# Attention, SwiGLU and four experts on one core: weight scaling, state decay, loads, first-stage order and last sums rearranged

## The chip, the cores and the metric

The kernel runs on one core of one Trainium2 chip. A core has five engines that work side by side, each through its own instructions in their order: PE (TensorE, matmuls, with its weight loads shown as PEld), DVE (VectorE), ACT (ScalarE), POOL (GpSimd) and SP (SyncE, which issues DMAs here). They wait for each other by semaphores. Data lies in DRAM, in on-chip SBUF (128 partitions) and in the eight banks of PSUM that PE adds into. The metric is the time of one execution on the device in microseconds (us), median of the runs.

## The reference

Three parts follow one another on 2 batches of 768 tokens with 384 channels (8 heads of 48), in float32:

```python
for t in range(S):                                   # attention with a decaying state
    state = alpha[:, :, t, :, None] * state + np.einsum('bhd,bhe->bhde', k[:, :, t], v[:, :, t])
    y[:, :, t] = np.einsum('bhd,bhde->bhe', q[:, :, t], state)

rms = np.sqrt(np.mean(x * x, axis=-1, keepdims=True) + 1e-06)
xn = x / rms * rms_g                                 # norm with a gain per channel
g = xn @ w_gate                                      # 384 x 1536
silu = g * (1.0 / (1.0 + np.exp(-g)))
x2 = silu * (xn @ w_val) @ w_out                     # 1536 x 384

p = domain_probs / (domain_probs.sum(-1, keepdims=True) + 1e-09)
for e in range(E):                                   # four experts, all of them used
    h = np.maximum(x2 @ w1[e], 0.0)                  # 384 x 1024
    out += p[:, e:e + 1] * (h @ w2[e])               # 1024 x 384
```

## The kernel before

**Products.** A float32 product is made of three matmuls in PE's faster format (`mm3`, L918 to L920): every operand is split into a high part (a rounded copy) and a low part (what is left), and low x high, high x high, high x low are added in one PSUM bank. So each weight and each intermediate needs a high copy (`whi`, `hh`, `x1h`, on ACT) and a subtraction (`wlo`, `hl`, `x1l`, on DVE).

**Attention.** Time is cut into six chunks c of 128 steps, for two batches b. Of a chunk the kernel loads alpha (`af`), k and q (`kq`, two DMAs of 224 KB, L617) and v, forms decay products by scans on DVE (`a_prep`, L652, L663, scaling the key at L679), scores on PE and a mask on DVE (`a_score`, L715, L724), the output (`a_y`, L735), the state S of each batch (`a_state`: the key's transpose L767, its copy `kdT` on ACT, the products L781, the decay of S by one DVE multiply, L812, and the addition, L807), and the norm without gain (`a_rms`), which leaves `x1h` and `x1l`.

**SwiGLU.** Tokens go in three blocks of 512 (`block1`). Of each block twelve steps f follow: a gate and a val product of nine matmuls each (`up1`, banks `g`, two of them), silu and the product with val, the split into `hh` and `hl`, and an output product of nine matmuls into three banks `o` (`outs`), one step behind. Block 0 needs chunks 0 and 1; its first four f run in two halves of 256 tokens, since chunk 1 is worked on at the same time. The last `outs` of a block comes directly behind the one before it.

**Weights.** Eighteen units of 128x768 (gate, val, out in turn, units u % 3 = 0, 1, 2) hold the SwiGLU weights. Each is loaded as 64-bit words (768 KB, L479, two buffers `raw`) and turned into float32 by three DVE operations (`w_conv`: L575, L583, L591, two buffers `cv`). `hilo_first` splits it: gate and val units are scaled by the gain `gneg` of the norm in three pieces on ACT (L514) and again in three pieces in the DVE subtraction (L526); out units need one ACT copy (L511) and one subtraction (L521). For units 0 to 2 the low part is made on PE instead (L543, L551) and copied by ACT (L558).

**Experts.** For each of four experts, three blocks and eight f: an up product (`e_up`, nine matmuls, banks `g` and `ph`), relu and split (L1266 on ACT, L1271 on DVE), a down product of nine matmuls into the three banks `o` (`e_down`). After f = 7 each bank is multiplied by the token's probability (L1314) and added to `acc` (L1322), in whole rows of 512 columns for experts 0 to 2, in halves of 256 for expert 3, which then stores each half from SP (L1330).

**Order.** A list scheduler (class `Plan`) sets the order of all engines' instructions when the program is built, from costs in us, handover times and a bias for each group of operations (`BIAS`); `MARGIN` and `SLIP` say when an operation may wait for a better one. Where the plan leaves PE idle ahead of the first dense product, `idle` (L1064 to L1070) puts in matmuls on zeros, of which there are 35 in groups of 20, 5, 5 and 5. The experts are planned with other, unchanged settings.

## Time and profile before

| | us |
|---|---|
| median of three runs | 706.62 (706.56 to 707.48) |
| the profiled execution | 706.30 |
| its span (first to last instruction) | 704.6 |
| PE busy | 688.9 (98%) |
| DVE busy | 323.9 (46%) |
| ACT busy | 199.2 (28%) |
| POOL busy | 13.0 (2%) |

Busy time counts an engine's work alone; an engine that waits in its order for a semaphore is idle. A timeline row gives the start in us from the span's start, the length in us, engine, line, operation, out<-in and the number of instructions that were put together; in brackets the idle time before it and what ended it. The length of a group reaches from the first start to the last end, and one matmul's or vector operation's length overlaps the next one's start, so the pace is read from the starts.

### The profile page before, as it was taken

How to read it: one execution, taken by the hardware profiler on the slowest of the kernel's cores; microseconds unless marked ns; L12 is line 12 of the kernel's file. 1: busy time of each engine (PE TensorE's matmuls, PEld its weight loads, DVE VectorE, ACT ScalarE, POOL GpSimd, SP SyncE). 2: the span in 40 equal slices, each digit the busy share in tenths (PEclk: the TensorE clock that was granted, in tenths of full speed). 3: DMA queues.
4: the chain of work that ended last, by engine and by line, in shares of the span. 5: the costliest groups of instructions: out<-in, count | busy, mean ns of one | idle time of the engine just before them, and what ended most of it. 6: DMA issues, size and time to landing. Idle time of an engine off the chain costs nothing. (4 is left out here: it accounts for less than half of the span.)

```text
span 704.6 us, 9312 instructions
## 1 busy us (share of the span) xinstructions
PE 688.9 (98%) x3877; PEld 570.7 (81%) x3877; DVE 323.9 (46%) x555; ACT 199.2 (28%) x407; POOL 13.0 (2%) x26
## 2 busy tenths in 40 slices
PE   8989999999999999999999999999999999999995
PEld 6889888778888888878888888888888888878784
DVE  7899999984223543431224413143313132231413
ACT  3754545443122443421113311113111111111110
POOL 1010000000000000000000000000000000000000
PEclk9999999999999999999999999999999999999999
DMA  9933554160000222320001210001000000000001
GB/s 260 268 130 116 172 183 151 61 214 1 1 1 2 91 93 87 124 100 1 16 0 60 93 57 16 0 16 45 16 1 15 1 15 1 16 22 23 30 16 47
DMA packets 21135, 45.16 MB, mean 64 GB/s; under 512 B 2160, under 2 KB 12192, under 8 KB 21088
## 3 DMA queue, kind: packets, MB, share of 16 engines
q1 hardware_dynamic: 20800, 44.49, 19.8%
q8 instruction: 31, 0.51, 0.3%
q14 instruction: 16, 0.13, 0.1%
q10 hardware_dynamic: 288, 0.03, 0.0%
HBM read 41.34 MB, written 3.17 MB: 63 GB/s over the span
## 5 line engine op out<-in xcount | busy, mean ns | idle before, releaser
L918 PE MATMUL o<-hl,whi 128*128 128x512 f32 (+1 forms) x408 | 158.0, 387 | 3.2 <-DVE acc L1322 1.6
L920 PE MATMUL o<-hh,wlo 128*128 128x512 f32 (+1 forms) x408 | 156.3, 383 | 0.0
L919 PE MATMUL o<-hh,whi 128*128 128x512 f32 (+1 forms) x408 | 156.2, 383 | 0.0
L918 PE MATMUL g<-x1l,whi 128*128 128x512 f32 (+1 forms) x384 | 146.5, 381 | 0.0
L920 PE MATMUL g<-x1h,wlo 128*128 128x512 f32 (+1 forms) x384 | 144.4, 376 | 0.0
L919 PE MATMUL g<-x1h,whi 128*128 128x512 f32 (+1 forms) x384 | 144.4, 376 | 0.0
L1271 DVE SCALAR_TENSOR_TENSOR hl<-g,hh 128x512 fp32r<-128x512 f32 x48 | 33.2, 691 | 146.0 <-ACT hh L1266 146.0
L918 PEld LDWEIGHTS o<-hl,whi 128*128 128x128 f32 x408 | 76.6, 188 | 20.7 <-PE ph L920 2.4
L920 PEld LDWEIGHTS o<-hh,wlo 128*128 128x128 f32 x408 | 76.6, 188 | 15.2
L919 PEld LDWEIGHTS o<-hh,whi 128*128 128x128 f32 x408 | 76.7, 188 | 14.4
L1271 DVE SCALAR_TENSOR_TENSOR hl<-ph,hh 128x512 fp32r<-128x512 f32 x48 | 33.1, 690 | 114.5 <-ACT hh L1266 114.4
L918 PEld LDWEIGHTS g<-x1l,whi 128*128 128x128 f32 x384 | 72.2, 188 | 14.0 <-DVE s L975 0.2
L920 PEld LDWEIGHTS g<-x1h,wlo 128*128 128x128 f32 x384 | 72.2, 188 | 13.3
L919 PEld LDWEIGHTS g<-x1h,whi 128*128 128x128 f32 x384 | 72.2, 188 | 12.7
L1266 ACT ACTIVATE hh<-g 128x512 fp32r<-128x512 f32 x48 | 28.7, 598 | 160.3 <-PE g L920 160.3
L1266 ACT ACTIVATE hh<-ph 128x512 fp32r<-128x512 f32 x48 | 28.7, 598 | 152.7 <-PE ph L920 152.7
L918 PE MATMUL ph<-x1l,whi 128*128 128x512 f32 x144 | 56.0, 389 | 0.0
L919 PE MATMUL ph<-x1h,whi 128*128 128x512 f32 x144 | 56.0, 389 | 0.0
L920 PE MATMUL ph<-x1h,wlo 128*128 128x512 f32 x144 | 56.0, 389 | 0.0
L975 DVE TENSOR_TENSOR s<-g,s 128x512 f32<-128x512 f32 (+1 forms) x40 | 25.4, 634 | 60.2 <-PE g L920 59.0
L493 DVE TENSOR_TENSOR wlo<-raw,whi 128x768 fp32r<-128x768 f32 x32 | 30.6, 956 | 20.4 <-ACT whi L488 20.1
L967 ACT ACTIVATE s<-g 128x512 f32<-128x512 f32 (+1 forms) x40 | 22.1, 552 | 53.0 <-PE g L920 52.6
(132 smaller groups left out, 606.1 us busy)
## 6 DMA issues: line engine op xcount, KB each, us to landing
raw<-in_w SPq DMA_DIRECT2D x34, 768.0 KB, 4.3
kq<-in_kq SPq DMA_DIRECT2D x20, 224.0 KB, 3.3
s<-p_dram SPq DMA_DIRECT2D x12, 256.0 KB, 3.5
out_y<-acc SPq DMA_DIRECT2D x18, 128.0 KB, 1.7
af<-in_af SPq DMA_DIRECT2D x10, 226.2 KB, 3.6
v<-in_v SPq DMA_DIRECT2D x10, 192.0 KB, 4.2
x_dram<-s SPq DMA_DIRECT2D x3, 256.0 KB, 3.3
raw<-x_dram SPq DMA_DIRECT2D x1, 768.0 KB, 4.2
```

The lines of the kernel that those rows point to most:

```text
L493: lambda: nc.vector.tensor_tensor(out=lo(), in0=src_ap(), in1=hi().bitcast(F32), op=ALU.subtract),
L918: nc.tensor.matmul(ps_ap, lhsT=lh, rhs=rl, start=first, stop=False)
L919: nc.tensor.matmul(ps_ap, lhsT=lh, rhs=rh, start=False, stop=False)
L920: nc.tensor.matmul(ps_ap, lhsT=ll, rhs=rh, start=False, stop=last)
L967: lambda: nc.scalar.activation(out=s()[:, :n], in_=pg()[:, :n], func=AF.Silu),
L975: lambda: nc.vector.tensor_mul(s()[:, :n], pv()[:, :n], s()[:, :n]), r=[pv], w=[s],
L1266: "ACT", 0.5, lambda: nc.scalar.activation(out=hh(), in_=ph(), func=AF.Relu),
L1271: lambda: nc.vector.scalar_tensor_tensor(out=hl(), in0=ph(), scalar=0.0, in1=hh().bitcast(F32), op0=ALU.max, op1=ALU.subtract,),
```

## The change

It has six parts.

1. The first plan has a bias for each step of each chunk (`00l` to `51y`: chunk, batch, and l, p, s, y, t or r for load, preparation, score, output, state and norm) and for each weight unit, other `MARGIN` and `SLIP`, other costs and start times. The order of the first stage becomes another. The fills are again 35, now in groups of 25, 5, 4 and 1, the first ahead of the first score.
2. Ten gate and val units (3, 4, 6, 7, 9, 10, 12, 13, 15, 16) are scaled in place on ACT before they are split; then one plain ACT copy makes the high part and one DVE subtraction the low part. Units 0 and 1 stay as they were, and buffers are tracked in halves.
3. The decay of the state is made by four ACT copies with a scale (112x96 each), for each of eight chunk-and-batch pairs, in place of one DVE multiply of 112x384.
4. k and q come in one DMA of 448 KB, but for chunk 0 of batch 0.
5. The first `e_up` is issued ahead of the last `outs` of block 2; from then on each down product follows its next up product, one step behind.
6. Expert 3 sums and stores in whole rows. Its last block has a sequence of its own (`e_end`): the third bank is closed after f = 4 and summed early; up products 6 and 7 follow; then f = 5 to 7 of the first two banks, with their sums and stores; then f = 5 to 7 of the third in two halves of 256 columns, in a `g` and a `ph` bank, each summed and stored, the last store from ACT's queue.

The diff, cut to its core (renamed keys, other costs and the table's entries are left out):

```diff
-BIAS = {"c00": -3016.7, "c01": -1212.5, "w0": 2486.8,
...
-MARGIN, SLIP = 0.00, 8.13
+BIAS = {'': -1198.5, '00l': -490.0, '00p': 390.6,
...
+MARGIN, SLIP = 8.75, 47.05
...
-            return 0.26 if b == "PE" else 0.2 if a == "PE" else 0.16
+            return 0.4 if b == "PE" else 0.2 if a == "PE" else 0.18
...
+    plan.FROM = {"SP": 0.7, "ACT": 3.3, "POOL": 2.4}
...
-        return plan.op("SP", max(0.6, mb / 0.36), fn, **kw)
+        return plan.op("SP", 0.25 + mb / 0.38, fn, **kw)
...
-        def his():
-            if not gains:
-                nc.scalar.activation(out=hi(), in_=t().bitcast(F32), func=AF.Copy)
-                return
+        def scaled(out):
             for k in range(KD):
                 nc.scalar.activation(
-                    out=part(hi(), k), in_=part(t().bitcast(F32), k), func=AF.Copy,
-                    scale=gneg[:, k : k + 1],
+                    out=part(out, k), in_=part(word(), k), func=AF.Copy, scale=gneg[:, k : k + 1]
                 )
-        def los():
...
-            for k in range(KD):
-                nc.vector.scalar_tensor_tensor(
-                    out=part(lo(), k), in0=part(t().bitcast(F32), k), scalar=gneg[:, k : k + 1],
-                    in1=part(hi().bitcast(F32), k), op0=ALU.mult, op1=ALU.subtract,
-                )
         if not by_pe:
-            plan.op("DVE", 1.0 if gains else 0.87, los, r=[t, hi], w=[lo])
+            if gains:
+                plan.op("ACT", 1.26, lambda: scaled(word()), r=key(t), w=key(t))
+            plan.op(
+                "ACT", 0.75, lambda: nc.scalar.activation(out=hi(), in_=word(), func=AF.Copy),
+                r=key(t), w=key(hi),
+            )
+            plan.op(
+                "DVE", 0.87,
+                lambda: nc.vector.tensor_tensor(
+                    out=lo(), in0=word(), in1=hi().bitcast(F32), op=ALU.subtract
+                ),
+                r=[*key(t), *key(hi)], w=key(lo),
+            )
+            return
...
+        if (c, b) == (0, 0):
...
+        else:
             dma(
-                0.23, lambda i=i: nc.sync.dma_start(out=t()[:HP, i], in_=kq[c, b, :, i]),
-                w=[(t, i)], chain=chain,
+                0.46, lambda: nc.sync.dma_start(out=t()[:HP], in_=kq[c, b]),
+                w=[(t, 0), (t, 1)], chain=chain,
             )
...
+        def scale():
+            for j in range(NP):
+                nc.scalar.activation(
+                    out=s()[:, j], in_=s()[:, j], func=AF.Copy,
+                    scale=p()[:, C + j * CS : C + j * CS + 1],
+                )
+
         if c:
-            plan.op(
-                "DVE", 0.47, lambda: nc.vector.tensor_mul(s(), s(), whole(2 * D)), r=[p],
-                w=[(s, 0), (s, 1)],
-            )
+            plan.op("ACT", 0.9, scale, r=[p], w=[(s, 0), (s, 1)])
...
-    def block1(steps, open_po=None):
+    def block1(steps, open_po=None, ahead=None):
...
+        if ahead:
+            ahead()
         outs(len(steps) - 1)
...
+    def e_end(e, blk):
+
+        e_up(e, blk, 5)
+        for d in range(KD):
+            e_prod(e, blk, 4, d, last=4 if d == 2 else 7)
+        e_sum(e, blk, 2)
+        e_up(e, blk, 6)
+        e_up(e, blk, 7)
+        for d, f in ((0, 5), (0, 6), (1, 5), (1, 6), (0, 7), (1, 7)):
+            e_prod(e, blk, f, d)
+            if f == 7:
+                e_sum(e, blk, d)
+                e_store(blk, d)
+        for c in halves:
+            pe[2] = h_bank()
+            for f in (5, 6, 7):
+                e_prod(e, blk, f, 2, c, first=5)
+            e_sum(e, blk, 2, c)
+            e_store(blk, 2, c, "ACT" if c.start else None)
...
+    for n in block1([(2, slice(0, 512), f) for f in range(12)], ahead=lambda: e_up(*es[0])):
...
-    for n, st in enumerate(es):
-        e_up(*st)
-        if n > 1:
-            if n == 2:
-                e_down(*es[0])
+    for n, st in enumerate(es[:-3]):
+        if n:
+            e_up(*st)
             e_down(*es[n - 1])
...
-    e_down(*es[-1])
+    e_end(E - 1, 2)
```

`e_prod` makes the three matmuls of one f and one bank, `e_sum` the multiplication and the addition of one bank, `e_store` the store.

Three places in the new order. The first is SP's queue in the first 25 us, where the first `raw` is weight unit 1 and the second unit 2, `wlo` and `whi` stand for chunk 1's alpha and v, and the later `af` and `kq` for chunk 2. Before:

```order
L479 DMA raw<-in_w 128x1536
L612 DMA wlo<-in_af 112x517
L628 DMA whi<-in_v 128x384
L612 DMA wlo<-in_af 112x517
L628 DMA whi<-in_v 128x384
L612 DMA af<-in_af 112x517 x2
L617 DMA kq<-in_kq 112x512
L479 DMA raw<-in_w 128x1536
L617 DMA x1h<-in_kq 112x512 x2
```

After:

```order
L480 DMA raw<-in_w 128x1536
L616 DMA wlo<-in_af 112x517
L639 DMA whi<-in_v 128x384
L616 DMA wlo<-in_af 112x517
L639 DMA whi<-in_v 128x384
L480 DMA raw<-in_w 128x1536
L616 DMA af<-in_af 112x517 x2
L627 DMA x1h<-in_kq 112x1024
```

Unit 2's load now stands ahead of chunk 2's loads, directly behind chunk 1's v. On DVE the three conversions of unit 0 (before L575, L583, L591) stand with one short operation between them; before, unit 1's first conversion stood ahead of the second, and a mask and two steps of the norm ahead of the third.

The second place is PE ahead of the first dense matmul (L918 before, L944 after). `g<-cv` and `g<-whi,nident` make the low part of units 0 to 2 in the g banks (`cv,ident` is unit 2), `att<-x1h` is the score of chunk 1, batch 0. Before:

```order
L543 MATMUL g<-cv,wlo 128x128 x3
L551 MATMUL g<-whi,nident 128x384
L1070 MATMUL o<-zw 128x512 x5
L715 MATMUL att<-x1h 128x128 x8
L543 MATMUL g<-cv,ident 128x128 x3
L551 MATMUL g<-whi,nident 128x384
L543 MATMUL g<-cv,ident 128x128 x3
L918 MATMUL g<-x1l,whi 128x256
```

After:

```order
L546 MATMUL g<-cv,wlo 128x128 x3
L554 MATMUL g<-whi,nident 128x384
L546 MATMUL g<-cv,ident 128x128 x3
L554 MATMUL g<-whi,nident 128x384
L546 MATMUL g<-cv,ident 128x128 x3
L728 MATMUL att<-x1h 128x128 x8
L944 MATMUL g<-x1l,whi 128x256
```

The split of unit 2 moves ahead of the score, and dense work follows the score directly.

The third place is DVE at the end of the program, from the last up products on. Before:

```order
L1271 SCALAR_TENSOR_TENSOR hl<-g,hh 128x512
L1271 SCALAR_TENSOR_TENSOR hl<-ph,hh 128x512
L1314 TENSOR_TENSOR o<-o,s 128x256
L1322 TENSOR_TENSOR acc_3728<-o,acc_3728 128x256
L1314 TENSOR_TENSOR o<-o,s 128x256 x3
L1322 TENSOR_TENSOR acc_3728<-o,acc_3728 128x256 x2
L1314 TENSOR_TENSOR o<-o,s 128x256 x2
L1322 TENSOR_TENSOR acc_3728<-o,acc_3728 128x256 x3
```

After:

```order
L1343 TENSOR_TENSOR o<-o,s 128x512
L1351 TENSOR_TENSOR acc_3726<-o,acc_3726 128x512
L1292 SCALAR_TENSOR_TENSOR hl<-g,hh 128x512
L1292 SCALAR_TENSOR_TENSOR hl<-ph,hh 128x512
L1343 TENSOR_TENSOR o<-o,s 128x512 x2
L1351 TENSOR_TENSOR acc_3726<-o,acc_3726 128x512 x2
L1343 TENSOR_TENSOR g<-g,s 128x256
L1343 TENSOR_TENSOR ph<-ph,s 128x256
L1351 TENSOR_TENSOR acc_3726<-g,acc_3726 128x256
L1351 TENSOR_TENSOR acc_3726<-ph,acc_3726 128x256
```

The third bank's first sum moves ahead of the last two `hl`, and behind them stand four whole-row and four half-row operations in place of twelve half-row ones.

## Rows read from the trace of the kernel before

**Rows 1.** Page, first part: busy us, share of the span and instructions of each engine.
```profile
PE 688.9 (98%) x3877; PEld 570.7 (81%) x3877; DVE 323.9 (46%) x555; ACT 199.2 (28%) x407; POOL 13.0 (2%) x26
```
**Rows 2.** Stretches: length, busy us of PE, PEld, DVE, ACT, POOL; last, GB/s.
```profile
0.00:31.20 31.20, 27.23 (x252) 22.66 (x252) 24.50 (x45) 16.44 (x48) 3.59 (x16) 1.00 0.92 265
31.20:130.00 98.80, 96.52 (x893) 83.54 (x893) 98.44 (x186) 49.74 (x129) 6.81 (x6) 1.00 0.45 146
```
**Rows 3.** PE's waits over the span: for whom, us in total, times, longest.
```profile
PE o L918 <- DVE acc L1322: 1.6, 2, 0.8
```
**Rows 4.** Timeline of PE around the first dense matmul.
```profile
28.41 1.16 PE L715 MATMUL att<-x1h 48*128 48x128 f32 x16 [0.73 <-DVE x1h L679]
...
31.20 0.38 PE L918 MATMUL g<-x1l,whi 128*128 128x256 f32 x1
```
**Rows 5.** Timeline of DVE, conversions of units 0 to 2 (the last row is unit 2's).
```profile
12.26 0.55 DVE L575 TENSOR_SCALAR cv<-raw 128x768 uint32<-128x768 uint32 x1
14.22 0.56 DVE L575 TENSOR_SCALAR cv<-raw 128x768 uint32<-128x768 uint32 x1 [1.40 <-DMA raw<-in_w]
...
16.95 0.95 DVE L591 SCALAR_TENSOR_TENSOR cv<-raw,cv 128x768 uint32<-128x768 uint32 x1
...
28.18 0.95 DVE L591 SCALAR_TENSOR_TENSOR cv<-raw,cv 128x768 uint32<-128x768 uint32 x1
```
**Rows 6.** Timeline of SP's queue: the load of unit 2.
```profile
18.06 1.21 SPq L479 DMA_DIRECT2D raw<-in_w  x1
```
**Rows 7.** Line 479 at 18 us, the same load: from issue to landing.
```profile
DMA to landing us min/median/max: 6.2/6.2/6.2
```
**Rows 8.** Line 628 from 8.5 to 9 us, chunk 1's second v load.
```profile
DMA to landing us min/median/max: 9.4/9.4/9.4
```
**Rows 9.** DVE's groups by shape: count, busy us, mean ns of one, idle before.
```profile
L526 DVE SCALAR_TENSOR_TENSOR wlo<-cv,gneg,whi 128x256 fp32r<-128x256 f32 x30 | 12.7, 480 | 0.0
...
L1314 DVE TENSOR_TENSOR o<-o,s 128x512 f32<-128x512 f32 x18 | 11.9, 690 | 0.0
...
L521 DVE TENSOR_TENSOR wlo<-cv,whi 128x768 fp32r<-128x768 f32 x5 | 4.8, 954 | 0.1
L812 DVE TENSOR_TENSOR S<-S,F 112x384 f32<-112x384 f32 x8 | 4.4, 552 | 0.0
```
**Rows 10.** ACT's groups by shape, columns as before.
```profile
L511 ACT ACTIVATE whi<-cv 128x768 fp32r<-128x768 f32 x6 | 5.1, 847 | 7.6 <-DVE cv L591 7.6
...
L558 ACT ACTIVATE wlo<-g 128x384 fp32r<-128x384 f32 x6 | 3.0, 499 | 0.6 <-PE g L551 0.6
...
L693 ACT ACTIVATE junk<-af 112x4 bf16<-112x4 f32 x10 | 2.1, 207 | 7.8 <-issue 6.0 <-DVE rms L849 0.8 <-ACT s L967 0.6
...
L1076 ACT ACTIVATE wlo<-ident,gneg 128x128 f32<-128x128 f32 x3 | 1.0, 385 | 0.0
```
**Rows 11.** Timeline of PE at the last output product of block 2.
```profile
300.27 0.50 PE L918 MATMUL o<-hl,whi 128*128 128x512 f32 x1 [0.41 <-DVE hl L985]
```
**Rows 12.** Timeline of PE where expert 3 goes from block 0 to 1.
```profile
632.92 0.39 PE L920 MATMUL ph<-x1h,wlo 128*128 128x512 f32 x1
634.10 0.47 PE L918 MATMUL o<-hl,whi 128*128 128x512 f32 x1 [0.79 <-DVE acc L1322]
...
635.45 0.39 PE L919 MATMUL o<-hh,whi 128*128 128x512 f32 x1
```
**Rows 13.** Timeline of PE, its last matmuls (seven in a row).
```profile
695.60 0.39 PE L920 MATMUL o<-hh,wlo 128*128 128x512 f32 x1
...
696.96 0.39 PE L920 MATMUL o<-hh,wlo 128*128 128x512 f32 x1
```
**Rows 14.** Timeline of DVE's last sums, the first and the last row.
```profile
696.02 0.43 DVE L1314 TENSOR_TENSOR o<-o,s 128x256 f32<-128x256 f32 x1 [1.40 <-PE o L920]
...
699.15 1.08 DVE L1322 TENSOR_TENSOR acc<-o,acc 128x256 f32<-128x256 f32 x3
```
**Rows 15.** Line 1330 from 700.4 us on, the last two stores.
```profile
DMA to landing us min/median/max: 1.8/2.2/2.6
```

More of the change, by code (lines that the diff above doesn't have):

```diff
@@ L158, in schedule @@
         ready = [0.0] * n
-        busy, cand, start = {}, {}, [None] * n
+        busy, cand, start = dict(self.FROM), {}, [None] * n
         for i in range(n):
@@ new lines, in hilo_first, with whole @@
+        if gains:
+            plan.op("ACT", 1.26, lambda: scaled(hi()), r=key(t), w=key(hi))
+        else:
+            plan.op(
+                "ACT", 0.75, lambda: nc.scalar.activation(out=hi(), in_=word(), func=AF.Copy),
+                r=key(t), w=key(hi),
+            )
+        for f in range(2):
+            p = gbank()
+            sl = slice(f * DM, (f + 1) * DM)
+            def whole(p=p, sl=sl):
+                for k in range(KD):
+                    c = slice(k * P, (k + 1) * P)
+                    nc.tensor.matmul(
+                        p()[:, c], lhsT=gdiag()[:, c] if gains else ident, rhs=word()[:, sl][:, c],
+                        start=k == 0, stop=False,
+                    )
+            plan.op("PE", 0.75, whole, r=[(t, f), gdiag], w=[p])
+            plan.op(
+                "PE", 0.2,
+                lambda p=p, sl=sl: nc.tensor.matmul(
+                    p()[:, :DM], lhsT=nident, rhs=hi()[:, sl], start=False, stop=True
+                ),
+                r=[(hi, f)], w=[p],
+            )
+            plan.op(
+                "ACT", 0.42,
+                lambda p=p, sl=sl: nc.scalar.activation(
+                    out=lo()[:, sl], in_=p()[:, :DM], func=AF.Copy
+                ),
+                r=[p], w=[(lo, f)],
+            )
@@ L578, in w_conv @@
             ),
-            r=[r], w=[t],
+            r=[r], w=key,
         )
@@ L586, in w_conv @@
             ),
[L587 removed]
+            r=[r], w=key,
         )
@@ L749, in go @@
                     inner(j, 1)
-            plan.op("PE", 1.73, go, r=[vt, *a, (Sp, 0), (Sp, 1), (t, 1)], w=[y])
+            plan.op(
+                "PE", 1.78, go,
+                r=[(vt, 0), *((x, n) for x in a for n in range(2)), (Sp, 0), (Sp, 1), (t, 1)], w=[y],
+            )
         else:
@@ L928, in dn_ops, with wr @@
         return tuple(t()[:, o + sl.start : o + sl.stop] for t in units[key])
-    def wr(u):
-        hi, lo = units[u]
-        return hi, lo, (lo, 0), (lo, 1)
+    def wr(u, f):
+        return [(t, f % 2) for t in units[u]]
     def u1(f, w):
@@ L957, in prod @@
             i = plan.op(
-                "PE", 9 * (n / 2400 + 0.0145), go, r=[*wr(u1(f, w)), *parts], w=[p], chain="dense"
+                "PE", 9 * (n / 2400 + 0.0145), go, r=[*wr(u1(f, w), f), *parts], w=[p], chain="dense"
             )
@@ L1288, in p_load, with parts, e_open, e_prod @@
         )
+    halves = (slice(0, 256), slice(256, 512))
+    def parts(t, cols, *key):
+        return [(t, *key, c.start) for c in halves if cols.start <= c.start < cols.stop]
+    def e_open(e, blk):
+        for d in range(KD):
+            pe[d] = obank()
+        p_load(e, blk)
+    def e_prod(e, blk, f, d, cols=slice(0, 512), first=0, last=7):
+        key = (19 + 4 * e + 2 * (f // 4), f // 2 % 2)
+        hh, hl = hq[e, blk, f]
+        p, n = pe[d], cols.stop - cols.start
+        def go():
+            mm3(
+                p()[:, cols], dn_ops(key, f, slice(d * P, (d + 1) * P)),
+                (hh()[:, cols], hl()[:, cols]), f == first, f == last,
+            )
+        plan.op(
+            "PE", 3 * (n / 2400 + 0.0133), go, r=[*units[key], hh, hl], w=parts(p, cols),
+            chain="dense",
+        )
@@ new lines, in e_sum @@
+    def e_sum(e, blk, d, cols=slice(0, 512)):
+        p, a, t, n = pe[d], acc[blk], pb[e, blk], cols.stop - cols.start
+        src, dst = parts(p, cols), parts(a, cols, d)
+        plan.op(
+            "DVE", 0.07 + n / 960,
+            lambda: nc.vector.tensor_mul(
+                p()[:, cols] if e else a()[:, d, cols], p()[:, cols], t()[:, cols]
+            ),
+            r=[t, *src], w=src if e else dst, port=False,
+        )
+        if e:
+            plan.op(
+                "DVE", 0.07 + n / 960,
+                lambda: nc.vector.tensor_add(a()[:, d, cols], p()[:, cols], a()[:, d, cols]),
+                r=src, w=dst, port=False,
+            )
@@ L1290, in e_down, with e_store @@
+    def e_store(blk, d, cols=slice(0, 512), queue=None):
+        a, rows, n = acc[blk], slice(d * P, (d + 1) * P), cols.stop - cols.start
+        go = lambda q: q.dma_start(
+            out=out[rows, blk * 512 + cols.start : blk * 512 + cols.stop], in_=a()[:, d, cols]
+        )
+        if queue:
+            plan.op("ACT", 0.1, lambda: go(nc.scalar), r=parts(a, cols, d))
+        else:
+            dma(n / 2000, lambda: go(nc.sync), r=parts(a, cols, d))
     def e_down(e, blk, f):
-        key = (19 + 4 * e + 2 * (f // 4), f // 2 % 2)
```

158 lines of the change are left out of this document (54 added, 104 removed).

## The prediction

> **What bounds the kernel now.** I began with the busy shares of the page [rows 1]: PE is busy for 98% of the span, DVE for 46%, ScalarE (ACT) for 28%. So only PE's idle time and the ends of the span can be won. The table by stretches then shows where they lie [rows 2]. Up to 31.2 us PE is busy for 27.23 us, but partly with matmuls on zeros; the first dense matmul starts at the end of that stretch. From 31.2 to 130 us, while attention chunks, weight conversion and dense work share the engines, PE works 96.52 of 98.80 us, DVE 98.44, ACT only 49.74: PE stands still for 2.28 us and DVE has nothing to spare. The list of PE's waits adds two waits of 1.6 us together for the accumulators' sums, which belong to the last expert [rows 3]. What follows PE's last matmul comes under "the end". This profiled execution took 706.30 us with a span of 704.6 (1.7 us lie outside); the median of the runs is 706.62, so I work the sum on 706.30 and add 0.32.
>
> **Start: -1.6 us.** Before, the score of chunk 1, batch 0 starts at 28.41, when DVE has written that chunk's key, and takes 1.16 us; weight unit 2's split on PE (L543, L551, L543) stands behind it, and only then, at 31.20, comes the first dense matmul [rows 4]. In the new order the split of unit 2 stands ahead of the score and the dense work behind it. If the score stays at 28.4, dense begins at 28.41 + 1.16 = 29.6, which is 1.6 earlier. This needs unit 2 converted before 28.4. Before, its last conversion starts at 28.18 [rows 5], because the raw weights are issued at 18.06 [rows 6] and land 6.2 us later, at 24.26 [rows 7]: the raw buffer is freed by unit 0's last conversion, which starts at 16.95 and ends about 17.9 [rows 5]. The change puts unit 0's three conversions almost together (the first began at 12.26, the third at 16.95), so that the buffer is free near 15, and moves unit 2's load on SP ahead of chunk 2's alpha and key loads. The transfers queued ahead of it end with a v load issued near 8.6 that took 9.4 us [rows 8], so 18.0; 768 KB (786 KB in decimal) at the 265 GB/s of this stretch [rows 2] are 3.0 us more: landing at about 21, 3 us earlier than now. Three conversions of 0.56, 0.95 and 0.95 us then end near 24 with other DVE work between them, well ahead of 28.4.
>
> Five more matmuls on zeros ahead of the first score, at 0.27 us each, hold that score back by up to 1.3 us. Behind it DVE masks the score and goes on to the weights, where it stands for 1.40 us on raw weights now [rows 5]: that wait covers the delay. Without that cover it would cost up to 1.3. One key-and-query load in place of two makes the first half arrive with the second, at most 224 KB / 265 GB/s = 0.85 us later; the same wait hides it at the start, and later loads run chunks ahead. Term: -1.6, from 0 (the score also slips) to -1.7.
>
> **DVE and ScalarE from 31 to 130 us: -1.0 us.** DVE loses, for ten units, three scaled subtractions of 480 ns against one plain subtraction of 954 ns: 10 x (1.44 - 0.95) = 4.9 us; and eight state decays of 552 ns, 4.4 us [rows 9]: 9.3 of 98.44 us. ScalarE keeps the thirty scalings, now in place, and gains ten plain copies of 847 ns (8.5 us). The decay becomes four activations of 112x96 with a scale from memory; no such row exists, so it is bounded by the 112x4 form at 207 ns and the 128x128 form with a scale at 385 ns [rows 10]. I take 0.33, because three of the latter took 1.0 us in a row and it is the nearest shape: 8 x 4 x 0.33 = 10.6 us, with ends 6.6 and 12.3. ACT goes from 49.7 to about 69 of 98.8 us and still has room.
>
> What is it worth? Relieving DVE can only return PE's idle time, 2.28 us at most. Against that, each converted unit now passes through one more ScalarE step: three scalings, then the high copy, then the subtraction. The step lengthens that unit's chain by 0.85 us, which the two-deep conversion buffers must hide. At the start of the dense part I expect one new wait: the first val product needs the g bank in which unit 2's second half was split, and that is released only after its copy to SBUF; such a copy takes 499 ns [rows 10], and I price the wait at 0.85, an estimate with a handover on either side. Of the idle 2.28 I let four fifths go, 1.85. Term: -1.85 + 0.85 = -1.0, with ends +1.0 (the extra step shows and old waits stay) and -2.3 (all idle time gone).
>
> A decay or scaling is a multiply, and the Trainium skill ("ScalarE: Activation LUTs", section "Rules for kernel authors") says that multiplies belong on VectorE, not ScalarE. The section "What ACT_TABLE_LOAD costs" gives 186 ns + 0.833 ns per column, about 93 more for a scale operand in memory, and about 93 of overlap in a row: an estimate of 0.27 us per activation, 1.1 us for four. The 385 ns of [rows 10] agree with it (386), and no run here shows the 112x96 form yet. By the rule the move loses time. By the rows it need not: VectorE is the full engine here and ScalarE the half empty one.
>
> **First expert product ahead of the last outs: -0.5 us.** At the end of block 2, PE stands 0.41 us before the matmul of 300.27, because hl is not ready [rows 11]; the next term shows that a stop costs more than its wait. With nine matmuls of the first expert put between, 2 us of work, hl is ready in time. Term: -0.5, ends -0.4 (the bare wait) and -0.6.
>
> **Whole-row sums of the last expert: -2.5 us.** At 634.10 PE has waited 0.79 for the accumulator's sum, and the five steps from 632.92 to 635.45 take 2.53 us [rows 12], where five at the usual pace of 0.227 (1.36 for six, [rows 13]) take 1.14: 1.4 lost, since the second bank opens late too. It happens twice [rows 3]. The sums are twelve half-row operations there, with hl in between; in whole rows they are six of 0.69 us [rows 9]. The list shows no third wait for a sum [rows 3], so the experts that sum in whole rows already have none. Term: -2.5, ends -1.6 (the bare waits) and -2.8.
>
> **The end: -1.9 us.** Now the first bank closes with the matmul of 695.60, the last with that of 696.96 [rows 13]; DVE begins its twelve half-row operations at 696.02, 0.42 after the first close, and ends at 699.15 + 1.08 = 700.23 [rows 14]. The span ends 4.35 later, at 704.57; in that lie the last store's issue and its landing, up to 2.6 us [rows 15]. After: two of the third bank's contributions (six matmuls, 1.36 us) move behind the other two banks, so the first bank closes at about 694.24 and DVE starts at 694.66. Half-row operations of 0.43 follow each other at 0.36 (1.08 for three), so they overlap by 0.07; four whole-row ones at 0.69 - 0.07 = 0.62 take it to 697.15. The third bank's remaining half-width matmuls take as long as whole ones did, PE ends as before, near 697.2, and four half-row operations at 0.36 bring DVE to 698.6, which is 1.65 earlier. The third bank's sum over f = 0 to 4 is made earlier, under PE's last up products. The last store has a queue of its own (ACT's) instead of waiting in SP's row; if it lands 1.8 rather than 2.6 later, 0.8 more is won. Term: -1.9, ends -1.65 and -2.45.
>
> **Sum.** -1.6 - 1.0 - 0.5 - 2.5 - 1.9 = -7.5: 706.30 - 7.5 = 698.8, and on the median's basis **699.1 us**. All favourable ends give -1.7 - 2.3 - 0.6 - 2.8 - 2.45 = -9.85, so 696.8; all unfavourable ones 0 + 1.0 - 0.4 - 1.6 - 1.65 = -2.65, so 704.0.
>
> **Rivals.**
> *The first 130 us give nothing back* (701.7). PE is what counts there, and a schedule that moves waits about may leave their total. Then only the last three terms hold, -4.9: 701.7. For it: DVE is full in every part of this stretch, so a wait removed in one place can appear in the next. Against it: 9.3 us of DVE work really go. Chance 0.2.
> *All of PE's idle time between 31 and 130 goes* and the end is at its favourable side: 706.62 - 9.85 = 696.8. For it: no wait in the list is long, and DVE's new slack is four times what is needed. Chance 0.13.
> *Unit 2's load does not come earlier, so the new start doesn't do what its order says.* The conversion of unit 2 now stands ahead of the first states and of chunk 1's scan on DVE; if the weights still land at 24.26, against the roughly 21 assumed, these wait too. Chunk 1's key slips by the same 3 us and dense begins near 31.2 + 1.3 = 32.5: -7.5 + 1.6 + 1.3 = -4.6, 702.0. Chance 0.07.
> *ScalarE's in-order queue becomes the bound, and the kernel is slower.* Ten extra copies and eight groups of four decays stand among silu, hh, x and kdT on one in-order engine, and every one of these feeds PE. If each of the 18 steps delays PE by its own length, 0.85 for a copy and 1.32 for four decays, that is 8.5 + 10.6 = 19.1 us, and with the -4.9 of the other parts 720.8. From about a quarter of that (4.9 / 19.1) it eats the whole gain. The Trainium skill's rule for multiplies points this way. Against it: ACT would still be idle for 30% of the stretch, and today its own waits there are for DVE and PE. Chance 0.05; a partial form of it, near no change, 0.04.
>
> **How the numbers follow.** The forecast, 699.1 with 697.6 to 700.9 as its own range, has 0.51; then 0.2, 0.13, 0.07 and 0.09 as above. The range for 8 in 10 reaches over the first rival and most of the third and stops where the second has half its weight: 696.9 to 702.7. A measurement can tell about 0.2% (1.4 us) from no change, so faster means below 705.2: everything but the last rival, 0.9; same 0.05; slower 0.05.
>
> **What would show each step.** Start: unit 2's raw weights landing near 21 and the first dense matmul near 29.6. In the stage to 130: DVE's busy time 9 us lower and below its stretch, ACT near 69 us, four decays in 1.0 to 1.5 us, PE's idle time near 1.3 us. No wait on hl at the end of block 2; no wait on acc between 630 and 670. At the end: the last sum ending about 1.4 us behind PE's last matmul instead of 2.9, and one store in ACT's queue. I am wrong if PE waits for ACT in the first 130 us for more than 2 us in all, or if the fill matmuls ahead of the first score push the whole start back.

## The result, and the profile after

The changed kernel takes 698.85 us (median of four runs, 696.62 to 699.97) against 706.59: a ratio of 0.989, 95% interval 0.9865 to 0.9914. The forecast was 699.1. The profiled execution took 699.97, with a span of 698.1 against 704.6 before. A second profiled execution of the same kernel, taken with the experiments, took 696.86 with a span of 695.1, and both are used below: single executions of this kernel differ by 3 us, the first profile is of the slowest of its four executions and the second of the fastest of its six, and the two tell where. Two executions of the experiments, of 1147 and 1768 us, lie far outside all others and are left out of every ratio and median below.

The busy shares of the first profile's page, as in [rows 1]:

```profile
PE 687.2 (98%) x3886; PEld 572.0 (82%) x3886; DVE 316.9 (45%) x513; ACT 215.8 (31%) x449; POOL 13.5 (2%) x26
```

Its table by stretches, as in [rows 2]:

```profile
0.00:31.20 31.20, 28.29 (x255) 23.47 (x256) 25.03 (x45) 17.37 (x49) 4.28 (x16) 1.00 0.86 263
31.20:130.00 98.80, 96.99 (x920) 84.54 (x920) 95.35 (x165) 63.69 (x162) 5.84 (x6) 1.00 0.49 152
```

PE stands still for 1.81 us between 31.2 and 130 us instead of 2.28 (in the second profile for 0.96). DVE's busy time over the whole span falls by 7.0 us, ACT's rises by 16.6. In this stretch DVE falls by 3.1 only, because it now does there part of what stood behind 130 us (from 130 to 300 us it falls from 79.7 to 75.4).

PE's waits over the span, first profile (for whom, us in total, times, longest):

```profile
PE o L1091 <- POOL zw L1073: 1.7, 1, 1.7
PE g L944 <- DVE s L1001: 0.9, 1, 0.9
PE att L889 <- ACT x L882: 0.7, 1, 0.7
PE att L802 <- ACT kdT L792: 0.5, 1, 0.5
PE att L908 <- DVE S L820: 0.4, 1, 0.4
PE g L944 <- ACT s L993: 0.3, 1, 0.3
```

The two waits for the accumulators [rows 3] and the wait for hl at the end of block 2 [rows 11] are gone; nothing is left behind 40 us. At the start, as in [rows 4], the timeline of PE shows the score and the first dense matmul:

```profile
29.63 1.16 PE L728 MATMUL att<-x1h 48*128 48x128 f32 x16
30.73 0.38 PE L944 MATMUL g<-x1l,whi 128*128 128x256 f32 x1
```

SP's, as in [rows 6], unit 2's load:

```profile
16.17 0.33 SPq L480 DMA_DIRECT2D raw<-in_w  x1
```

DVE's, as in [rows 5], unit 0's last conversion, unit 2's first, and chunk 1's key:

```profile
15.18 0.96 DVE L594 SCALAR_TENSOR_TENSOR cv<-raw,cv 128x768 uint32<-128x768 uint32 x1
...
21.95 0.56 DVE L578 TENSOR_SCALAR cv<-raw 128x768 uint32<-128x768 uint32 x1 [1.08 <-DMA raw<-in_w]
...
28.89 0.69 DVE L691 TENSOR_TENSOR x1h<-x1h,wlo 112x512 f32<-112x512 f32 x1
```

Unit 2's load is issued at 16.17, when unit 0's last conversion ends, lands at 21.86, and its first conversion follows it at once; the key of chunk 1 is ready at 29.58 and the first dense matmul starts at 30.73.

DVE's last rows, as in [rows 14]; PE's last matmul ends at 691.91:

```profile
689.12 1.38 DVE L1343 TENSOR_TENSOR o<-o,s 128x512 f32<-128x512 f32 x2 [2.08 <-PE o L946]
690.41 1.28 DVE L1351 TENSOR_TENSOR acc<-o,acc 128x512 f32<-128x512 f32 x2
...
692.62 0.41 DVE L1351 TENSOR_TENSOR acc<-ph,acc 128x256 f32<-128x256 f32 x1
```

DVE ends 1.1 us behind PE instead of 2.9. The table puts the stations of the program side by side, all read from the timelines (us; "block 1 ends" is the start of the first copy of its result, L1027 before, L1056 after; new and old order are those of the first stage):

| profile | unit 2 lands | first dense | block 1 ends | PE ends | DVE ends | span |
|---|---|---|---|---|---|---|
| before | 24.26 | 31.20 | 227.13 | 697.35 | 700.23 | 704.6 |
| changed | 21.86 | 30.73 | 225.25 | 691.91 | 693.03 | 698.1 |
| changed, second profile | 20.88 | 29.75 | 223.34 | 690.05 | 691.17 | 695.1 |
| new end only | 23.54 | 30.61 | 226.49 | 693.42 | 694.66 | 698.6 |
| new end, work moved, old order | 23.36 | 30.39 | 226.40 | 693.47 | 694.71 | 698.6 |
| both moves undone, new order | 20.89 | 29.76 | 228.66 | 695.41 | 696.53 | 700.6 |
| decay undone | 21.86 | 30.73 | 225.47 | 692.18 | 693.31 | 697.4 |
| gain undone | 21.77 | 30.65 | 227.63 | 694.38 | 695.50 | 699.6 |
| decay twice | 20.37 | 29.24 | 224.15 | 690.83 | 691.96 | 697.0 |
| 20 fills | 21.56 | 30.42 | 224.02 | 690.75 | 691.88 | 695.9 |
| 20 fills, halves | 20.67 | 29.54 | 223.14 | 689.90 | 691.02 | 694.9 |
| 14 fills, halves | 20.77 | 29.63 | 223.23 | 689.92 | 691.05 | 696.0 |

From the first dense matmul to the end of block 1 (column 4 less column 3) it is 195.93 before and 194.52 and 193.59 in the two profiles of the changed kernel. The row with both moves undone holds 3.4 us at the lower TensorE clock, of which more under experiment 6. Between the two profiles the spans differ by 3.0: 0.98 at the start, 0.93 in this stretch, and the rest behind DVE's end, where the last store landed 3.4 us after its issue in one and 2.3 in the other.

### The profile page after: what moved, and what is told of

The parts are those of the page before. It is cut to its first block, busy times and chain, and to the rows that moved or that the text cites. A ratio compares the mean times of both kernels' runs of the same rounds, so it can differ in the third digit from the quotient of the medians.

```text
span 698.1 us, 9281 instructions
## 1 busy us (share of the span) xinstructions
PE 687.2 (98%) x3886; PEld 572.0 (82%) x3886; DVE 316.9 (45%) x513; ACT 215.8 (31%) x449; POOL 13.5 (2%) x26
## 4 chain that ended last, share of the span: by engine, by line
PE 96%; DVE 2%; DMA 1%; issue 0%; POOL 0%; DVEq 0%; POOLq 0%
PE o L944 13%; PE o L946 13%; PE o L945 13%; PE g L944 12%; PE g L946 12%; PE g L945 12%; PE ph L944 5%; PE ph L946 5%; PE ph L945 5%; PE att L751 2%; PE att L728 2%; PE o L1099 1%; DMA raw<-in_w 1%; PE att L802 1%; PE att L889 1%; DVE cv L586 1%
## 5 line engine op out<-in xcount | busy, mean ns | idle before, releaser
L944 PE MATMUL o<-hl,whi 128*128 128x512 f32 (+1 forms) x405 | 156.2, 386 | 0.0
L944 PE MATMUL g<-x1l,whi 128*128 128x512 f32 (+1 forms) x384 | 146.7, 382 | 1.2 <-DVE s L1001 0.9
L944 PEld LDWEIGHTS o<-hl,whi 128*128 128x128 f32 x405 | 76.1, 188 | 15.7
L944 PEld LDWEIGHTS g<-x1l,whi 128*128 128x128 f32 x384 | 72.2, 188 | 15.1 <-DVE s L1001 1.1
L945 PEld LDWEIGHTS g<-x1h,whi 128*128 128x128 f32 x384 | 72.3, 188 | 12.7
L944 PE MATMUL ph<-x1l,whi 128*128 128x512 f32 x144 | 56.0, 389 | 0.0
L1001 DVE TENSOR_TENSOR s<-g,s 128x512 f32<-128x512 f32 (+1 forms) x40 | 25.3, 633 | 55.3 <-PE g L946 55.0
L494 DVE TENSOR_TENSOR wlo<-raw,whi 128x768 fp32r<-128x768 f32 x32 | 30.6, 956 | 20.4 <-ACT whi L489 20.1
L993 ACT ACTIVATE s<-g 128x512 f32<-128x512 f32 (+1 forms) x40 | 22.1, 553 | 54.3 <-PE g L946 54.3
```

Source lines behind the costliest of these rows:

```text
L494: lambda: nc.vector.tensor_tensor(out=lo(), in0=src_ap(), in1=hi().bitcast(F32), op=ALU.subtract),
L944: nc.tensor.matmul(ps_ap, lhsT=lh, rhs=rl, start=first, stop=False)
L945: nc.tensor.matmul(ps_ap, lhsT=lh, rhs=rh, start=False, stop=False)
L993: lambda: nc.scalar.activation(out=s()[:, :n], in_=pg()[:, :n], func=AF.Silu),
L1001: lambda: nc.vector.tensor_mul(s()[:, :n], pv()[:, :n], s()[:, :n]), r=[pv], w=[s],
```

## The experiments

Each ratio is to the kernel before, which ran among the same set; the changed kernel in the second set gives 0.9885 (0.9867 to 0.9902), 697.66 us.

**1. The new end alone.** The kernel before with the first expert product ahead of the last outs, whole-row sums and `e_end`; the first plan as it was.

```diff
-        if n > 1:
-            if n == 2:
-                e_down(*es[0])
+        if n:
+            e_up(*st)
             e_down(*es[n - 1])
...
+    e_end(E - 1, 2)
```

> The first plan (order, weight scaling, decay, loads) is that of the kernel before; only the first expert product ahead of the last outs, the whole-row sums and the new last block are added. My theory: these parts bring 0.6 + 2.8 + 1.0 to 1.9 us, so 701.3 to 702.2, and the first 130 us bring the other 2 to 3 us of the change. Rival: the first 130 us give nothing back, and this kernel is as fast as the changed one, about 698.9.

Measured: 700.88 us, ratio 0.994 (0.9926 to 0.9955). By the ratios the new end brings 0.6% or about 4.2 us and the first stage the rest of the change's 1.1%, 3.5 to 3.9 us. The theory gave the new end 4.4 to 5.3 us; the medians of the set (705.65 before) give 4.8, the ratio a little less than its lower end. The rival, that the first stage brings nothing, falls: the interval lies above both of the changed kernel's.

**2. 20 matmuls on zeros instead of 25, and 3. also the second key and query load in halves, and 4. 14 of them with the halves.** The order of everything else stays.

```diff
-        for n in range(max(0, round(gap / 0.22)) if start else 0):
+        for n in range(max(0, min(20, round(gap / 0.22))) if start else 0):
```

```diff
-            0.46, lambda: nc.sync.dma_start(out=t()[:HP], in_=kq[c, b]),
+            for i in (1, 0):   # chunk 0, batch 1 alone
+                nc.sync.dma_start(out=t()[:HP, i], in_=kq[c, b, :, i])
```

> The changed kernel with 20 instead of 25 matmuls on zeros ahead of the first score; every other instruction stands where it stood. Theory: the five cost the start what they last, 1.1 to 1.4 us, because unit 0's conversions follow the first mask on DVE, free the raw buffer later and so hold unit 2's load: without them the load issues near 14.9 instead of 16.2, the first dense matmul comes near 29.5 instead of 30.7, and the time is about 697.6. Rival: the five are covered by the wait for unit 2's weights, which land when the DMAs queued ahead allow: first dense matmul at 30.7 again, time 698.9.

> 20 instead of 25 matmuls on zeros, and the key and query of chunk 0, batch 1 in two loads again; the order stays. With 20 fills alone the first dense matmul came at 30.42, since DVE then stood 0.79 us for the single 448 KB load, which landed 7.0 us after its issue where the halves had landed after 5.0 and 5.4. Theory: fills and single load each hold the first mask, and with both gone the mask starts near 10.6 and the first dense matmul comes near 29.5; time 0.8 to 1.2 us below the changed kernel. Rival: the conversion buffers (freed by PE's split of unit 0) or unit 2's weights hold the start anyway: no difference above 0.3 us.

> 14 matmuls on zeros ahead of the first score (25 in the changed kernel) and the second key and query load in halves. Theory: the first score then starts when its key is ready, near 9.2, the mask near 10.4 and the first dense matmul near 29.0 us; the time is 0.5 to 1.0 us below the changed kernel. Rival: with fewer matmuls PE keeps its slow pace (0.43 us for 512 columns, seen until 4 to 7 us) further into the first stage, and what the score gains is lost in the products behind it: dense at 29.5 or later, no gain.

Measured: 698.38, 698.03 and 697.91 us; ratios 0.990 (0.9884 to 0.9916), 0.9883 (0.9865 to 0.9901) and 0.9874 (0.9856 to 0.9891). None can be told from the changed kernel, though each interval leaves room for about 1 us. The theories of 2 and 4 put the first dense matmul at 29.5 and 29.0 us, and it came at 30.42 and 29.63. That of 3 put it at 29.5, and it came at 29.54, but the changed kernel's second profile has 29.75 with 25 fills and the single load. In the timeline of SP with 14 fills the load of unit 2 is issued 1.2 us earlier than in the changed kernel's first profile:

```profile
14.98 0.33 SPq L480 DMA_DIRECT2D raw<-in_w  x1
```

In the same run DVE still waits for it before unit 2's first conversion:

```profile
20.86 0.56 DVE L578 TENSOR_SCALAR cv<-raw 128x768 uint32<-128x768 uint32 x1 [1.17 <-DMA raw<-in_w]
```

And PE's first dense matmul there:

```profile
29.63 0.39 PE L948 MATMUL g<-x1l,whi 128*128 128x256 f32 x1
```

It lands at 20.77, near the 20.88 of the changed kernel's second profile, where it was issued 0.74 us later. Issued between 14.98 and 16.31, that load landed between 20.4 and 21.9 in the profiles of the new order, 4.6 to 6.3 us after its issue. And the first dense matmul follows the landing by 8.86 to 8.88 us in all the rows of the table with the new order. So unit 2's landing sets the start, since DVE converts unit 2 ahead of chunk 1's key; the fills and the single load act on it only through the raw buffer, and only in part. (In the run with halved sums below it was 10.07. There PE waited 1.4 us for the norm's x, and its clock then fell to the lower level from 25.2 to 28.6 us, while it split weight units.) No cost of the fills shows beyond this spread; the rival of 3 holds as far as it allows. The rival of 4 has the number (29.5 or later) but not the reason: with 14 fills PE's faster pace began at 5.0 us, before the first score of 8.96.

The single 448 KB load does cost DVE something, as the run with 20 fills shows:

```profile
9.85 0.69 DVE L684 TENSOR_TENSOR kq<-kq,F 112x512 f32<-112x512 f32 x1 [0.79 <-DMA kq<-in_kq]
```

It had landed 7.0 us after its issue where the halves landed after 5.0 and 5.4 in the profile of before. With 25 fills no profile shows more than 0.43 us of that wait.

**5. The old end.** The last block in the plain sequence, with whole-row sums and stores from SP.

```diff
-    for n, st in enumerate(es[:-3]):
+    for n, st in enumerate(es):
...
-    e_end(E - 1, 2)
+    e_down(*es[-1])
```

> The changed kernel with its last block in the plain sequence (up 7, down 6, down 7, three whole-row sums, three stores from SP). Theory: DVE ends 1.0 to 1.8 us later behind PE's last matmul, and the time is 0.9 to 1.9 us above the changed kernel: 699.8 to 700.8. Rival: the last store's landing takes what it takes and hides the earlier sums: 698.9, no difference.

Measured: 699.31 us, ratio 0.9912 (0.9895 to 0.9928), 0.2 to 0.3% or 1.6 to 1.9 us behind the changed kernel by the ratios, though the intervals overlap. In its trace DVE ends 2.4 us behind PE's last matmul (1.1 with `e_end`, 2.9 before). PE's last row:

```profile
689.91 0.39 PE L946 MATMUL o<-hh,wlo 128*128 128x512 f32 x1
```

DVE's last row:

```profile
691.46 1.28 DVE L1351 TENSOR_TENSOR acc<-o,acc 128x512 f32<-128x512 f32 x2
```

So of the 1.75 us that DVE's end moved, whole rows account for 0.4 and `e_end` for 1.3. That part of the theory holds. Whether the landing hides a part of it, as the rival has it, the times do not settle.

**6. Both moves undone, 7. the decay alone, 8. the gain alone,** each at its place in the new order, with PE's and SP's order untouched.

```diff
         def scale():
-            for j in range(NP):
-                nc.scalar.activation(
-                    out=s()[:, j], in_=s()[:, j], func=AF.Copy,
...
+            nc.vector.tensor_mul(s(), s(), whole(2 * D))
```

```diff
-                plan.op("ACT", 1.26, lambda: scaled(word()), r=key(t), w=key(t))
+                plan.op("ACT", 1.26, lambda: None, r=key(t), w=key(t))
...
+            for k in range(KD):   # in the DVE operation, for units with a gain
+                nc.vector.scalar_tensor_tensor(
+                    out=part(lo(), k), in0=part(word(), k), scalar=gneg[:, k : k + 1],
...
```

> The changed kernel with the gain in DVE's subtraction again (three scaled pieces) and the state's decay as one DVE multiply again, at the same places of the order; ScalarE loses its ten plain copies and 32 decay pieces. Theory: DVE is busy for 96.95 of 100.4 us from 29.6 to 130 us, so 9.3 us more do not fit; some 6 us come out as waits of PE, unless PE's own slack takes them: 702 to 705. Rival (PE alone sets the stage, ScalarE's added steps cost as much as DVE's relief): within 1 us of the changed kernel, 698 to 700.

> The decay alone on DVE again, at the same places: DVE +4.4 us, ScalarE -9.3 us of work. Both moves undone cost about 4.5 us (702.91 with some 698.4 for the changed kernel). Theory: DVE has 3.45 us free from 29.6 to 130 us, so one move alone costs less than its half: +0.5 to +1.8 us. Rival: DVE's order is tight everywhere and every microsecond comes through: +2 to +2.5 us.

> The gain alone in DVE's subtraction again, at the same places: DVE +4.9 us, ScalarE -8.5 us of work and one step less for ten units. Theory, as for the decay: +0.5 to +1.8 us, because free time takes part of it. Rival: it comes through in full with the units' chain: +2.5 us; or the shorter chain outweighs the longer subtraction, and the time falls.

Measured: 702.44 us, 0.9964 (0.995 to 0.9978); 699.71, 0.9912 (0.9893 to 0.993); 700.68, 0.9923 (0.9906 to 0.9939). By the ratios to the changed kernel's 0.9885 that is +5.6 us, +1.9 and +2.7 (to its 0.989, 0.4 less each); the interval of the second overlaps the changed kernel's. From the first dense matmul to the end of block 1 the traces give 198.90, 194.74 and 196.98 against 193.59 and 194.52. The work on DVE comes back as waits of PE, between 28 and 140 us, in the run with both:

```profile
PE g L953 <- DVE s L1010: 1.0, 2, 0.6
PE att L815 <- ACT kdT L805: 0.7, 1, 0.7
PE o L953 <- DVE hl L1020: 0.5, 2, 0.3
PE att L741 <- PE g L955: 0.4, 1, 0.4
```

The same stretch as above there:

```profile
31.20:130.00 98.80, 95.47 (x876) 82.46 (x876) 97.31 (x182) 48.17 (x126) 4.95 (x6) 0.98 0.45 142
```

PE idles 3.3 us and ACT half of the time, while DVE is busy for 97.31 of 98.80 us. The granted clock (third column from the end) is 0.98 here, and two stretches show why:

```profile
50.00:54.00 4.00, 3.20 (x29) 2.48 (x28) 3.92 (x10) 1.29 (x6) 0.00 (x0) 1.00 0.63 215
54.00:57.40 3.40, 3.40 (x37) 3.17 (x37) 3.40 (x8) 1.25 (x3) 0.00 (x0) 0.50 0.00 0
```

PE stood still for 0.80 of 4 us, and then its clock was at the lower of its two levels, 1.2 GHz, for 3.4 us, in which it had no idle time. Half of these, 1.7 us, is the most that this adds to the stretch, so that at least 2.7 to 3.6 of its 4.4 to 5.3 us are left for waits. The time does not hang on it: two other executions with a mean granted clock of 0.999, too high for such a fall (it alone takes 0.0024 off the mean), took 702.36 and 703.38. So in this order the two moves are worth 5.2 to 5.6 us by the times, and DVE's work comes through to PE. The expectation for both holds; no trace shows an execution of this kernel in which the clock did not fall. The decay alone costs 0.2 to 1.2 us by the stretch and 1.9 by the times, at the edge of what the theory gave; the gain alone costs 2.5 to 3.4 by the stretch, in full, as its rival had it.

**9. The moved work in the old order.** Experiment 1 with the gain in place on ACT and the decay on ACT, each where its operation stood.

```diff
-                    out=part(hi(), k), in_=part(t().bitcast(F32), k), func=AF.Copy,
-                    scale=gneg[:, k : k + 1],
+                    out=part(hi() if by_pe else t().bitcast(F32), k),
+                    in_=part(t().bitcast(F32), k), func=AF.Copy, scale=gneg[:, k : k + 1],
                 )
+            if not by_pe:
+                nc.scalar.activation(out=hi(), in_=t().bitcast(F32), func=AF.Copy)
...
-            plan.op("DVE", 0.47, lambda: nc.vector.tensor_mul(s(), s(), whole(2 * D)), ...
+            plan.op("DVE", 0.47, scale, r=[p], w=[(s, 0), (s, 1)])
```

> The kernel before with the new end (as in the run with the new end only, 700.88), in the old order of the first stage, but with the gain applied in place on ScalarE and the decay as four ScalarE copies, each issued at the place where its operation stood. From the first dense matmul to the end of block 0 the old order took 111.0 us with the work on DVE; the new order takes 113.2 us with the work on DVE and 107.9 to 108.8 with it on ScalarE. Theory: the moved work brings the gain in either order, as DVE is the full engine: 108.5 to 110 us for the stretch, time 698.5 to 700. Rival: the gain comes from order and work together, and in the old order ScalarE's added steps cost as much as DVE's relief brings: 110.5 to 112 us, time 700.5 to 702.

Measured: 700.02 us, ratio 0.990 (0.9886 to 0.9915), against 700.88 and 0.994 for the same kernel without the moves. The times put the gain at 0.9 us (medians) to 2.8 (ratios). The traces show none of it: both spans are 698.6, and from the first dense matmul to the end of block 1 they take 196.01 and 195.88. DVE is relieved in the trace, and PE stands still no less:

```profile
31.20:130.00 98.80, 95.93 (x897) 83.01 (x896) 93.67 (x161) 62.20 (x160) 6.46 (x6) 1.00 0.46 148
```

DVE has 5.1 us free there and PE still idles 2.9. Its waits went elsewhere, as the list of that run shows:

```profile
PE att L717 <- DVE rms L855: 0.7, 2, 0.4
PE att L783 <- ACT kdT L773: 0.6, 1, 0.6
PE att L869 <- ACT x L862: 0.6, 1, 0.6
PE g L924 <- DVE s L981: 0.4, 1, 0.4
```

How much the moves are worth in the old order stays open, between nothing and 2.8 us. What the traces show is that neither half suffices: the moves in the old order leave the stretch at 196.0, the new order with the work on DVE makes it 198.9 (at least 197.2 without the fall of the clock), and both together 193.6 to 194.5.

**10. Half-row sums in expert 3 again,** in blocks 0 and 1.

```diff
-                e_sum(e, blk, d)
-                if e == E - 1:
-                    e_store(blk, d)
+                for c in halves if e == E - 1 else (slice(0, 512),):
+                    e_sum(e, blk, d, c)
+                    if e == E - 1:
+                        e_store(blk, d, c)
```

> The changed kernel with the sums and stores of expert 3's blocks 0 and 1 in halves of 256 columns again; the last block stays. Theory: PE waits for acc twice, about 0.8 us, and loses about 1.4 us each time: +2.5 to +2.8 us, 700.2 to 701.5. Rival: the waits came from the old lag of the down products behind the up products, and in the new loop the halves cost nothing: 697.7 to 698.9.

Measured: 701.44 us, ratio 0.9925 (0.9905 to 0.9944), 2.5 to 2.8 us above the changed kernel. The waits are back, 1.3 us in two, in PE's list:

```profile
PE o L944 <- DVE acc L1351: 1.3, 2, 0.7
```

In PE's timeline the first stands where [rows 12] had it:

```profile
632.59 0.47 PE L944 MATMUL o<-hl,whi 128*128 128x512 f32 x1 [0.66 <-DVE acc L1351]
```

From block 2's last copy to PE's end the trace is 2.0 us longer (391.83 against 389.81), somewhat less than the times say; the mechanism holds. The fall of the clock near 25 us, told above, lies ahead of this stretch.

**11. ScalarE's decay doubled,** four more copies of the same form behind each group, into a tile that nothing reads.

```diff
+            for j in range(NP):
+                nc.scalar.activation(
+                    out=more[:HP, : 2 * D], in_=ident[:HP, : 2 * D], func=AF.Copy, scale=mhalf[:HP],
+                )
```

> The changed kernel with four more ScalarE copies (112x96, into a tile that nothing reads) behind each of the eight decays: ScalarE's work from 29.6 to 130 us goes from 64 to about 73 of 100.4 us. Theory: ScalarE has room, and PE loses less than 1 us: 697.7 to 699.7. Rival: ScalarE's in-order queue is the bound, and each group delays PE by its 1.2 us: +4 to +10 us.

Measured: 700.26 us, ratio 0.9919 (0.9897 to 0.994), 2.4 us above the changed kernel by the ratios, with a wide spread (698.86 to 703.66) and an interval that overlaps the changed kernel's; in the trace, which is of the fastest of the six, the stretch to the end of block 1 takes 194.91, 0.4 to 1.3 us more. ScalarE's bound as the rival meant it (1.2 us for each of eight groups) does not show. The added copies were busy for 11.9 us, and 0.05 to 0.3 us of each group come through, so they need not be free, although ScalarE's busy share in the changed kernel is 64%.

## Why the prediction held, step by step

**Start, forecast -1.6.** Measured: -0.47 in the first profile, -1.45 in the second. The landing of unit 2 was right (about 21; it was 21.86 and 20.88). Wrong was the step "if the score stays at 28.4". I took the key of chunk 1 for fixed and asked only that unit 2 be converted before it. But the new DVE order puts these conversions and the first states ahead of chunk 1's scan, so that the key hangs on unit 2's landing: 21.9 + 7.7 = 29.6 for the score, +1.1 for dense. My third rival had this chain, but only for a load at the old time. With it the sum is 21 + 8.87 = 29.9, or -1.3. The fills' cover was half right: the first score did slip by 1.41 (9.12 to 10.53; 0.97 in the second profile) and unit 2's issue to 16.17 instead of 15, but experiments 2 to 4 show no cost of that beyond the spread of the landing.

**31 to 130 us, forecast -1.0.** Measured, to the end of block 1: -1.41 and -2.34. The two sizes behind it were off. The three scaled subtractions overlap: 30 of them were busy for 12.7 us [rows 9], not 30 x 0.48, so the gain's move frees 12.7 - 9.5 = 3.2 us of DVE and not 4.9; with the decay 7.6; 0.9 more in the sums and 0.3 less elsewhere make the page's fall of 7.0. And three of the eight decays stand behind 130 us, before and after, so that the stretch itself was relieved of 5.0 us and not 9.3. ACT rose there to 63.69 us, not 69. On ScalarE the groups by shape of the changed kernel give the moved work its durations:

```profile
L521 ACT ACTIVATE whi<-cv 128x768 fp32r<-128x768 f32 x15 | 12.6, 842 | 3.3 <-DVE cv L594 3.2
L833 ACT ACTIVATE S<-S,F 112x96 f32<-112x96 f32 x32 | 9.3, 363 | 1.6 <-DVE S L828 1.6
```

The 32 decay pieces are busy for 9.3 us, 0.29 each in a row, between the bounds and near the 0.33 taken. The 363 ns of one agree with the Trainium skill's formula ("ScalarE: Activation LUTs", section "What ACT_TABLE_LOAD costs"), which gives an estimate of 186 + 93 + 0.833 x 96 = 359. Its rule that multiplies belong on VectorE (section "Rules for kernel authors") speaks the other way than experiments 6 to 8: here the same work on VectorE costs 5.2 to 5.6 us more by the times, with VectorE busy for 97.31 of 98.80 us. The new wait for the first val product came, smaller than 0.85: PE lost 0.46 there, 0.3 of it in the wait for `s` L993 above; a larger one (0.9, for `s` L1001) that I did not foresee came near 38 us. And the reason I gave, DVE's relief returning PE's idle time, is only half of it: by experiment 9 the trace of the old order returns nothing for it.

**Ahead of the last outs, -0.5.** The wait is gone, and from the end of block 1 to the last copy of block 2's result (302.64 before, 302.10 after) it takes 76.85 us against 75.51, less the 2.04 of the nine matmuls that moved in: -0.7.

**Whole-row sums, -2.5.** Both waits are gone; from that copy to PE's end it is 389.81 us against 394.71, and 2.04 of the difference are the moved matmuls: -2.9. Experiment 10 gives 2.0 to 2.8 back.

**The end, -1.9.** DVE's end came nearer to PE's by 1.75, as worked out (1.65); PE's end to the span's end shrank from 7.22 to 6.19 in the first profile and to 5.05 in the second. The difference is the last store's landing, the term I had left between 1.8 and 2.6.

**The sum** was -7.5; the profiles give -6.5 and -9.5 and the medians -7.7. The size came out right because two errors cancel: a start forecast too well, and a first stage too poorly, and because the three terms at the end (-4.9 forecast; -4.6 in the first profile, 0.6% or 4.2 us measured alone) were read from waits that the trace showed whole. That the median came within 0.3 us of the forecast is luck beyond that: single executions differ by 3 us.

## What to carry to other kernels

Ask of a moved operation not only whether it is early enough for its own reader, but what now stands behind it in its engine's order: here a weight load 8.9 us upstream came to set the start. Moving work off a full engine pays when the order is made for it; the same move in the old order moved PE's waits and showed no gain in the trace. Two of the runs show PE's clock fall after it had stood still, so look at the granted clock of a stretch before its loss is put down to waits alone. Where single executions differ by more than a term, compare stretches between two fixed stations of the program instead of spans.

## What the runs showed of the hardware beyond expectation

The matmuls on zeros at the start run at two paces, and the step between them comes at another time in each execution. PE's timeline of the changed kernel, first profile, 25 of them:

```profile
3.10 7.50 PE L1099 MATMUL o<-zw 128*128 128x512 f32 x25
```

And in the second:

```profile
3.10 7.05 PE L1099 MATMUL o<-zw 128*128 128x512 f32 x25
```

In the single rows they start 0.43 us apart until 6.5 us in the first and 5.7 in the second, and 0.21 to 0.23 apart from then on; over the profiles of all the runs the last slow one starts between 4.0 and 6.9 us. The column of the granted clock (third from the end) reads 1.00, the higher level of 2.4 GHz, in the slow part too; two stretches of the first profile:

```profile
3.00:7.00 4.00, 4.00 (x11) 3.11 (x11) 3.02 (x5) 2.20 (x8) 0.19 (x1) 1.00 0.95 283
7.00:10.00 3.00, 3.00 (x15) 2.62 (x14) 2.66 (x5) 1.42 (x6) 0.00 (x0) 1.00 1.04 325
```

PE had been idle until 1.66 us. The first score starts 0.44 us apart in the two. A distance of 0.427 is 512 columns at the lower level, 1.2 GHz, so the pace and that column disagree. The trace settles it: its records of the granted clock begin with the rise to 1.00, at 6.93 us in the first profile and at 6.01 in the second, and the pace changes at the same moments, as in all fourteen profiles (rises at 4.5 to 7.5 us). Ahead of its first record the column is not a reading. The Trainium skill ("TensorE: Matmul & The Clock Gate", "Part 1: The HAM clock gate") tells of a start at the lower clock and of a rise whose moment differs between runs; the pace and the records agree with it. What sets the moment was not tried.

The clock also fell within two runs, both times after PE had stood still: for 0.80 of the 4 us ahead in the run with both moves undone, for 1.82 of 4 in the run with halved sums. The rows of the latter:

```profile
21.20:25.20 4.00, 2.18 (x18) 1.55 (x18) 3.22 (x7) 2.21 (x6) 0.00 (x0) 1.00 0.96 281
25.20:28.60 3.40, 3.40 (x27) 3.31 (x28) 3.34 (x6) 2.07 (x5) 0.00 (x0) 0.50 0.72 243
```

The same load takes a different time in each execution: unit 2's 768 KB landed 4.6 to 6.3 us after the issue in the profiles of the new order, and the last store of 128 KB from ACT's queue 2.3 to 3.4 us. Of the 3.0 us between the two profiles of the changed kernel, 0.53 are unit 2's load and 1.1 the last store. Another 0.45 is the issue of unit 2's load (15.72 against 16.17), as much as the 25 fills ended apart: the clock rose 0.92 us later in the first profile.
